# Linear attention with complex decay before a mixture of experts: the state increment computed transposed, two heads in two column halves

## The chip, the cores and the metric

The kernel runs on one core of one Trainium2 chip. The metric is the device time of one execution, in microseconds (us); several executions are taken, and the median is given. Lower is better.

## What is computed

For 4 sequences (B) of 768 steps (S) and 8 heads (H) of width 48 (D), a complex state of 48x48 per head decays and takes in an outer product at each step, and a query reads its real part. The result, 3072 rows of 384 numbers, then goes through four experts with weights per row.

```python
mag = np.sqrt(a_re * a_re + a_im * a_im)
scale = np.minimum(mag, 0.999) / (mag + 1e-06)
a_re_n, a_im_n = (a_re * scale, a_im * scale)
for t in range(S):
    ar, ai = (a_re_n[:, :, t, :, None], a_im_n[:, :, t, :, None])
    new_re = ar * S_re - ai * S_im
    new_im = ar * S_im + ai * S_re
    kv = np.einsum('bhd,bhe->bhde', k[:, :, t], v[:, :, t])
    S_re, S_im = (new_re + kv, new_im)
    y[:, :, t] = np.einsum('bhd,bhde->bhe', q[:, :, t], S_re)
...
for e in range(E):
    h = np.maximum(x @ w1[e], 0.0)
    out += p[:, e:e + 1] * (h @ w2[e])
```

All data is fp32, and there are 3072 rows, 384 columns, 1024 hidden units per expert.

## The kernel before

The work has two parts that overlap in time. The rows are cut into 12 groups (g) of 256 steps, three for each sequence, and each group into two chunks (c) of 128 steps.

**Attention, per group.** VectorE normalises the decays (`norm`), forms their running products (`prefix`) and from them Q and K, the queries and keys scaled by these products (`finish`). Q and K go to DRAM and come back in another layout as `Qst` and `Kst` (SyncE's queue), with the real part in partitions 0 to 47 and the imaginary part from 64 on (M = 112 partitions, 16 between them zero). Then, per chunk, the function `chunk` hands out pieces:

- `increment`: what the chunk adds to the state. K of the chunk (one tile for the real, one for the imaginary part, i) is turned by six transposes on TensorE into `ktp` (L399), evicted by ScalarE into `KT` (L400), and multiplied with the values `vc`, one product per head, into `dp` (L404), in PSUM. The old state less `dp` is the new state `G` (L407 for the first chunk of a sequence, L409 otherwise). The last chunk of a sequence has no increment, so there are 20.
- `scores`: `Kst` times `Qst`, eight heads in two tiles `sc` (L416), masked on VectorE into `scs` (L419).
- `values`: state times queries (L428) plus scores times values (L432), into `yp`; here two heads stand in one PSUM tile, one in partitions 0 to 47, one from 64 on, which is to say that their products use two column halves of the array. ScalarE evicts `yp` (L438).

`rotate` (L450 to L453) multiplies the state by the group's whole decay on VectorE, ready for the next group.

`attention` is a generator that strings these pieces together and yields twice before its last one: increment and scores of chunk 0; its values and the scores of chunk 1; then the values of chunk 1, the store of y to DRAM and its load as the next input `xa`, the increment of chunk 1, and `rotate`.

**Experts.** Two of the four (E1) run in the first part, on the group before (`moe1`, in eight steps f2 of two blocks of 128 hidden units each). A step multiplies with the first weights into `ph` (L147), evicts it as a rounded part `hh` on ScalarE (L154) and a remainder `hl` on VectorE (L155), and multiplies those with the second weights into `po` (L164), one step later. The input is split likewise into `xha` (ScalarE, L136) and `xla` (VectorE, L137). The other two experts run in a second part on all rows (`phb` L568, `pob` L581), after the attention is done.

**What sets the order.** A scheduler orders the instructions of each engine by its own estimates of time. The program's text gives the priorities: `between` takes the next piece of `attention` at steps k of the experts' loop, and `first` says from which on. Instructions under `keep_in_program_order` stay in the order of the text. PSUM tiles of the attention (`ktp`, `dp`, `sc`, `yp`) share four buffers, tag `pa`.

Of the kernel before, what the change touches and what calls it, by code (L numbers as in the profile page):

```python
# [8 lines left out]
F32 = mybir.dt.float32  # L9
F32R = mybir.dt.float32r  # L10
AF = mybir.ActivationFunctionType
ALU = mybir.AluOpType
# [3 lines left out]
B, H, S, D = 4, 8, 768, 48  # L16
HD = H * D
NT = B * S
E, F = 4, 1024
P = 128  # L20
# [3 lines left out]
CG = G // C  # L24
# [9 lines left out]
M = 112  # L34
IM = 64
# [24 lines left out]
def fast_path(ctx, tc, qkP, aP, vP, probsP, w, out, flag):  # L60
# [134 lines left out]
    with ExitStack() as c1:  # L195
# [18 lines left out]
        KT = big.tile([P, H, M], F32, name="KT")  # L214
# [5 lines left out]
        nc.gpsimd.memset(KT, 0.0)  # L220
# [163 lines left out]
        def chunk(g, c, K, y):  # L384
# [8 lines left out]
            def increment():  # L393
                if last:
                    return
                for i in range(2):
                    kt_ps = ps_a.tile([P, HD], F32, tag="pa", name=f"ktp{g}_{c}_{i}")
                    for j in range(NJ):
                        nc.tensor.transpose(kt_ps[:, j * P:(j + 1) * P], K[:, i, j * CG + c, :], ident)  # L399
                    nc.scalar.activation(KT[:, :, i * IM:i * IM + D],  # L400
                                         kt_ps.rearrange("p (h d) -> p h d", d=D), AF.Copy)
                d_ps = ps_a.tile([M, H, D], F32, tag="pa", name=f"dp{g}_{c}")
                for h in range(H):
                    nc.tensor.matmul(d_ps[:, h, :], KT[:, h, :], vc[:, h * D:(h + 1) * D], start=True, stop=True)  # L404
                Gt = small.tile([M, H, D], F32, tag="G", name=f"G{g}_{c}")
                if first:
                    nc.scalar.activation(Gt, d_ps, AF.Copy, scale=-1.0)  # L407
                else:
                    nc.vector.tensor_tensor(Gt, state[g, c], d_ps, op=ALU.subtract)  # L409
                state[g, c + 1] = Gt  # L410
# [29 lines left out]
            return increment, scores, values  # L440
# [15 lines left out]
        def attention(g, K):  # L456
            y = small.tile([M, HP, G], F32, tag="y", name=f"y{g}")
            (inc0, sc0, val0), (inc1, sc1, val1) = (chunk(g, c, K, y) for c in range(CG))
            inc0()
            yield sc0()  # L460
            if g == 0:
                sc1()
            val0()
# [8 lines left out]
            inc1()  # L472
            rotate(g)
            yield x
# [41 lines left out]
        x = {0: split_x(0, [r for r in attention(0, K.pop(0))][-1])}  # L516
        for g in range(NG + 1):
            if g == NG:
                check_all()
            if g >= 1:  # L520
# [3 lines left out]
                def between(k, g=g, pieces=pieces, first=first):  # L524
                    if first <= k < first + 3:
                        r = next(pieces, None)
                        if r is not None:
                            x[g] = r
# [278 lines left out]
```

## Time and profile before

| | us |
|---|---|
| median of three runs | 1034.55 (1033.19 to 1038.9) |
| the profiled execution, its own time | 1037.87 |
| its span in the trace | 1036.2 |
| PE busy in the span | 995.4 |
| DVE busy | 597.5 |
| ACT busy | 360.6 |
| increments (L404), PE busy, x320 | 35.7 |
| transposes of K (L399), PE busy, x120 | 19.1 |
| eviction into KT (L400), ACT busy, x40 | 18.4 |
| subtraction into G (L409), DVE busy, x16 | 8.9 |
| scores (L416), PE busy, x384 | 54.5 |
| values (L428 and L432), PE busy, x320 and x384 | 32.1 and 36.1 |

PE is TensorE's multiplying, PEld its loading of weights, which overlaps; DVE is VectorE, ACT ScalarE, POOL GpSimd, SP SyncE. Rows of matmuls count passes: a product of two fp32 operands shows as two records, a transpose as one. A record's duration includes the way through the array, so several overlap, and the distance between starts tells what one costs. Rows of a timeline give start, duration, engine, line, operation, tiles (output <- inputs), operand sizes and a count of merged records; in square brackets the idle time before, with what ended it.

### The profile page before, as it was taken

Reading aid. Unit: us, or ns where it says so; the run is one execution under the profiler, and the core shown is the slowest. Engines: PE = TensorE matmul, PEld = TensorE weight load, DVE = VectorE, ACT = ScalarE, POOL = GpSimd, SP = SyncE. Lnnn points to the kernel's source line nnn. Section 1 sums busy time; section 2 is a strip of 40 time slices with the busy share of each in tenths; the row PEclk is TensorE's granted clock in tenths of the full one; section 3 lists DMA queues with packets and bytes.
Section 4 is the critical chain, followed back from the end, with each engine's and each line's share of the span. In section 5 each row is a group of like instructions: output and inputs, shape, how many; then the busy total and the mean of one; then the engine's idle time right before and its main releaser. Section 6 shows DMA issues by size and latency. Waiting matters only on the chain.

```text
span 1036.2 us, 15971 instructions
## 1 busy us (share of the span) xinstructions
PE 995.4 (96%) x6522; PEld 926.2 (89%) x6522; DVE 597.5 (58%) x1195; ACT 360.6 (35%) x647; POOL 25.2 (2%) x47
## 2 busy tenths in 40 slices
PE   5689999899999999999999999999999999999996
PEld 3469899898999999999999999999999999999996
DVE  6688888797978898888982264232232232321221
ACT  7745345262534626355342254121111111111110
POOL 4000000000000000000000000000000000000000
PEclk9689999899999999999999999999999999999999
DMA  8826373564638455483652493012030010100000
GB/s 281 206 100 139 110 203 112 149 160 116 182 111 206 121 147 150 118 212 119 146 132 68 130 358 123 1 38 85 1 109 14 23 70 1 61 1 1 31 1 34
DMA packets 80722, 113.12 MB, mean 109 GB/s; under 512 B 5440, under 2 KB 66032, under 8 KB 80640
## 3 DMA queue, kind: packets, MB, share of 16 engines
q1 hardware_dynamic: 78368, 102.40, 35.8%
q0 software_dynamic: 2272, 9.62, 2.6%
q8 instruction: 53, 0.87, 0.4%
q14 instruction: 29, 0.24, 0.1%
HBM read 74.11 MB, written 37.88 MB: 108 GB/s over the span
## 4 chain that ended last, share of the span: by engine, by line
PE 84%; DMA 7%; DVE 5%; ACT 2%; issue 1%; DVEq 0%; POOL 0%; SPq 0%; ACTq 0%; POOLq 0%
PE pob L581 19%; PE phb L568 19%; PE ph L147 16%; PE po L164 15%; PE sc L416 5%; DMA Kst<-k_d 2%; PE yp L432 2%; PE lp L123 2%; PE dp L404 2%; PE yp L428 2%; DMA k_d<-K 2%; PE ktp L399 1%; DMA xa<-y_d 1%; DMA pr<-probsP 1%; DMA y_d<-y 1%
## 5 line engine op out<-in xcount | busy, mean ns | idle before, releaser
L574 DVE SCALAR_TENSOR_TENSOR hlb<-phb,hhb 128x512 fp32r<-128x512 f32 x96 | 66.3, 691 | 245.5 <-ACT hhb L573 245.5
L573 ACT ACTIVATE hhb<-phb 128x512 fp32r<-128x512 f32 x96 | 57.4, 598 | 313.3 <-PE phb L568 299.1
L164 PE MATMUL po<-wlo,hh 128*128 128x384 f32 x384 | 129.4, 337 | 0.0
L581 PE MATMUL pob<-wlo,hhb 128*128 128x384 f32 x384 | 129.3, 337 | 0.0
L164 PE MATMUL po<-whi,hh 128*128 128x384 f32 x384 | 129.1, 340 | 0.0
L581 PE MATMUL pob<-whi,hhb 128*128 128x384 f32 x384 | 128.9, 336 | 0.0
L164 PE MATMUL po<-whi,hl 128*128 128x384 f32 x384 | 123.6, 338 | 0.6 <-DVE hl L155 0.6
L581 PE MATMUL pob<-whi,hlb 128*128 128x384 f32 x384 | 117.8, 336 | 0.0
L154 ACT ACTIVATE hh<-ph 128x512 fp32r<-128x512 f32 x96 | 57.2, 596 | 158.2 <-PE ph L147 154.8
L147 PE MATMUL ph<-xha,whi 128*128 128x256 f32 x576 | 105.0, 290 | 5.3 <-ACT xha L136 5.3
L147 PE MATMUL ph<-xha,wlo 128*128 128x256 f32 x576 | 104.2, 287 | 0.0
L147 PE MATMUL ph<-xla,whi 128*128 128x256 f32 x576 | 102.7, 286 | 0.0
L155 DVE SCALAR_TENSOR_TENSOR hl<-ph,hh 128x512 fp32r<-128x512 f32 x96 | 66.0, 688 | 54.6 <-ACT hh L154 54.2
L147 PEld LDWEIGHTS ph<-xha,whi 128*128 128x128 f32 x576 | 87.6, 194 | 6.3 <-ACT xha L136 5.7
L568 PE MATMUL phb<-xhb,whi 128*128 128x512 f32 x288 | 91.8, 392 | 0.0
L147 PEld LDWEIGHTS ph<-xha,wlo 128*128 128x128 f32 x576 | 85.1, 194 | 0.4 <-issue 0.4
L147 PEld LDWEIGHTS ph<-xla,whi 128*128 128x128 f32 x576 | 83.9, 193 | 0.7 <-issue 0.7
L568 PE MATMUL phb<-xlb,whi 128*128 128x512 f32 x288 | 83.4, 392 | 0.0
L568 PE MATMUL phb<-xhb,wlo 128*128 128x512 f32 x288 | 82.1, 393 | 0.0
L581 PEld LDWEIGHTS pob<-wlo,hhb 128*128 128x128 f32 x384 | 72.1, 188 | 3.5
L581 PEld LDWEIGHTS pob<-whi,hhb 128*128 128x128 f32 x384 | 72.1, 188 | 3.4
L164 PEld LDWEIGHTS po<-whi,hh 128*128 128x128 f32 x384 | 72.6, 189 | 0.2 <-issue 0.2
(201 smaller groups left out, 1576.2 us busy)
## 6 DMA issues: line engine op xcount, KB each, us to landing
wst<-w SPq DMA_DIRECT2D x32, 384.0 KB, 5.2
qk<-qkP SPq DMA_DIRECT2D x24, 384.0 KB, 7.1
acc_d<-acc POOLq DMA_DIRECT2D x24, 384.0 KB, 4.4
prev<-acc_d SPq DMA_DIRECT2D x24, 384.0 KB, 4.8
q_d<-Q SPq DMA_DIRECT2D x22, 387.0 KB, 4.1
Qst<-q_d SPq DMA_DIRECT2D x22, 387.0 KB, 6.0
A<-aP SPq DMA_DIRECT2D x22, 384.0 KB, 8.4
k_d<-K SPq DMA_DIRECT2D x22, 384.0 KB, 2.9
```

The lines of the kernel that those rows point to most:

```text
L123: nc.tensor.matmul(lp, ident, src[:, us], start=True, stop=False)
L147: ins = nc.tensor.matmul(ph[:, u, :], wt[:, j * P:(j + 1) * P], xt[:, j, :], start=(n == 0), stop=(n == 3 * NJ - 1))
L154: nc.scalar.activation(hh, ph, AF.Relu)
L155: nc.vector.scalar_tensor_tensor(hl, ph, 0.0, hh, op0=ALU.max, op1=ALU.subtract)
L164: nc.tensor.matmul(po[t], ht[:, u, t * P:(t + 1) * P], wt[:, HD:], start=(i % FE == 0 and n == 0), stop=(i % FE == FE - 1 and n == 2))
L404: nc.tensor.matmul(d_ps[:, h, :], KT[:, h, :], vc[:, h * D:(h + 1) * D], start=True, stop=True)
L416: nc.tensor.matmul(s_ps[:, h, :], Kc[:, hf * 4 + h, :], Qc[:, hf * 4 + h, :], start=True, stop=True)
L428: ins = nc.tensor.matmul(yo, state[g, c][:, h, :], Qc[:, h, :], start=True, stop=False)
L568: nc.tensor.matmul(ph, wt[:, j * P:(j + 1) * P], xt[:, j, :], start=(n == 0), stop=(n == 3 * NJ - 1))
L573: nc.scalar.activation(hh, ph, AF.Relu)
L574: nc.vector.scalar_tensor_tensor(hl, ph, 0.0, hh, op0=ALU.max, op1=ALU.subtract)
L581: nc.tensor.matmul(po[t], ht[:, t * P:(t + 1) * P], wt[:, HD:], start=(i % FE == 0 and n == 0), stop=(i % FE == FE - 1 and n == 2))
```

## The change

The increment changes sides. Before, K was the operand that is loaded into the array (128 steps by 112 columns: real part, zeros, imaginary part) and the head's values streamed (48 columns); the result stood as the state does, d in partitions, e along the row. Now the values are loaded (48 columns), and K streams, 48 real and 48 imaginary columns of a head side by side; the result is the transposed increment. Two heads share a PSUM tile, one in partitions 0 to 47 and one from 64 on, like the values' products. ScalarE evicts both halves into a tile `dT`, and four transposes on TensorE, one per head pair, turn it into `zp`, from which the subtraction reads.

The transposes and the subtraction are a piece of their own, `turn`: for chunk 0 it comes after the scores, for chunk 1 after one more `yield`, so that a group now takes four steps of the experts' loop (`first + 4`) instead of three, with `rotate` in the fourth.

```diff
-        KT = big.tile([P, H, M], F32, name="KT")
+        KT = big.tile([P, 2, HD], F32, name="KT")
+        dT = big.tile([M, HP, 2, IM], F32, name="dT")
...
-        nc.gpsimd.memset(KT, 0.0)
+        nc.gpsimd.memset(dT, 0.0)
...
-                    nc.scalar.activation(KT[:, :, i * IM:i * IM + D],
-                                         kt_ps.rearrange("p (h d) -> p h d", d=D), AF.Copy)
-                d_ps = ps_a.tile([M, H, D], F32, tag="pa", name=f"dp{g}_{c}")
-                for h in range(H):
-                    nc.tensor.matmul(d_ps[:, h, :], KT[:, h, :], vc[:, h * D:(h + 1) * D], start=True, stop=True)
+                    nc.scalar.activation(KT[:, i], kt_ps, AF.Copy)
+                d_ps = ps_a.tile([P, HP, 2, D], F32, tag="pa", name=f"dp{g}_{c}")
+                for p in range(HP):
+                    for u, h in enumerate((2 * p, 2 * p + 1)):
+                        ins = nc.tensor.matmul(d_ps[u * IM:u * IM + D, p], vc[:, h * D:(h + 1) * D],
+                                               KT[:, :, h * D:(h + 1) * D], start=True, stop=True)
+                        if p or u:
+                            tc.keep_in_program_order(ins)
+                for u in range(2):
+                    us = slice(u * IM, u * IM + D)
+                    nc.scalar.activation(dT[us, :, :, :D], d_ps[us], AF.Copy)
+
+            def turn():
+                if last:
+                    return
+                z_ps = ps_a.tile([M, HP, P], F32, tag="pa", name=f"zp{g}_{c}")
+                for p in range(HP):
+                    nc.tensor.transpose(z_ps[:, p, :M], dT[:, p].rearrange("q c d -> q (c d)")[:, :M], ident[:M, :M])
+                zv = z_ps.rearrange("q p (u e) -> q (p u) e", u=2)[:, :, :D]
                 Gt = small.tile([M, H, D], F32, tag="G", name=f"G{g}_{c}")
                 if first:
-                    nc.scalar.activation(Gt, d_ps, AF.Copy, scale=-1.0)
+                    nc.scalar.activation(Gt, zv, AF.Copy, scale=-1.0)
                 else:
-                    nc.vector.tensor_tensor(Gt, state[g, c], d_ps, op=ALU.subtract)
+                    nc.vector.tensor_tensor(Gt, state[g, c], zv, op=ALU.subtract)
...
             inc0()
             yield sc0()
             if g == 0:
                 sc1()
+            turn0()
             val0()
...
             inc1()
+            yield x
+            turn1()
             rotate(g)
-            yield x
+            yield None
...
-                    if first <= k < first + 3:
+                    if first <= k < first + 4:
```

Since the scheduler places the instructions anew, others move too. Three places follow; a row is line, operation, output <- inputs, size and count, and lines of the changed kernel from L399 on stand one, later up to 18 lines further down.

On PE, around the scores of group 2, chunk 0, which run among the expert steps of group 1 (the number after `hh`, `hl` and `ph` is the step f2). Before:

```order
L164 MATMUL po_0_1_1347<-whi_420,hh_3_1477 128x384
L164 MATMUL po_0_1_1347<-wlo_421,hh_3_1477 128x384
L404 MATMUL dp_0_1433<-v_0_1419,KT 112x48 x8
L416 MATMUL sc_0_0_1444<-Qst,Kst 128x128 x4
L416 MATMUL sc_0_1_1451<-Qst,Kst 128x128 x4
L428 MATMUL yp_0_1493<-Qst,G_1_1111 48x128 x2
L164 MATMUL po_0_1_1347<-whi_420,hl_3_1478 128x384
L147 MATMUL ph_5_1594<-xha_1152,whi_473 128x256 x3
```

and with the change:

```order
L164 MATMUL po_0_1_1376<-wlo_370,hh_1_1396 128x384
L164 MATMUL po_0_1_1376<-whi_369,hl_1_1397 128x384
L405 MATMUL dp_0_1462<-KT,v_0_1448 48x96 x3
L431 MATMUL sc_0_0_1473<-Qst,Kst 128x128 x4
L431 MATMUL sc_0_1_1480<-Qst,Kst 128x128 x4
L147 MATMUL ph_3_1487<-xha_1181,whi_408 128x256 x3
L147 MATMUL ph_3_1487<-xha_1181,wlo_409 128x256 x3
L147 MATMUL ph_3_1487<-xla_1182,whi_408 128x256 x3
```

The scores stand behind step 3's second product before, and behind step 1's now; the eight increments are cut into five (further up) and three, with the experts' `po` between.

On PE, ahead of the values of group 8, chunk 0. Before:

```order
L164 MATMUL po_0_1_4503<-whi_368,hh_1_4523 128x384
L164 MATMUL po_0_1_4503<-wlo_369,hh_1_4523 128x384
L164 MATMUL po_0_1_4503<-whi_368,hl_1_4524 128x384
L428 MATMUL yp_0_4614<-Qst,G_1_4191 48x128 x2
L432 MATMUL yp_0_4614<-scs_0_0_4570,v_0_4540 48x128 x2
L428 MATMUL yp_0_4614<-Qst,G_1_4191 48x128 x2
```

and with the change:

```order
L164 MATMUL po_0_1_4602<-wlo_370,hh_1_4622 128x384
L164 MATMUL po_0_1_4602<-whi_369,hl_1_4623 128x384
L418 MATMUL zp_0_4713<-ident,dT 112x112 x4
L443 MATMUL yp_0_4720<-Qst,G_1_4331 48x128 x2
L447 MATMUL yp_0_4720<-scs_0_0_4669,v_0_4639 48x128 x2
L443 MATMUL yp_0_4720<-Qst,G_1_4331 48x128 x2
```

The four transposes `zp` stand directly ahead of the values; the products that they turn were issued before the two tiles of scores, one whole `ph` and `po` further up.

On DVE, at the start of the experts on group 0. `xla` is the input's remainder for the first expert step, `hl_0` that step's eviction; `sk_16`, `fm1` and `A` belong to `prefix` of group 1, `Q` to its `finish`, `s` is a sum of squares in it, and `G` with `P` is `rotate`. Before:

```order
L453 TENSOR_TENSOR G_1_660<-G_1_660,P_163 112x384
L137 TENSOR_TENSOR xla_667<-xa_639,xha_666 128x768
L266 TENSOR_TENSOR A_187<-sk_16a,sk_16b 128x3x16
L267 TENSOR_TENSOR A_187<-sk_16a,sk_16b 128x3x16
L262 TENSOR_TENSOR fm1a<-A_187 128x651
L264 TENSOR_TENSOR fm1a<-A_187 128x651
L263 TENSOR_TENSOR fm1b<-A_187 128x651
L265 TENSOR_TENSOR fm1b<-A_187 128x651
L155 SCALAR_TENSOR_TENSOR hl_0_806<-ph_0_786,hh_0_805 128x512
L266 TENSOR_TENSOR A_187<-fm1a,fm1b 128x21x31
L267 TENSOR_TENSOR A_187<-fm1a,fm1b 128x21x31
L155 SCALAR_TENSOR_TENSOR hl_1_831<-ph_1_811,hh_1_830 128x512
```

and with the change:

```order
L263 TENSOR_TENSOR fm1a<-A_188 128x651
L265 TENSOR_TENSOR fm1a<-A_188 128x651
L264 TENSOR_TENSOR fm1b<-A_188 128x651
L266 TENSOR_TENSOR fm1b<-A_188 128x651
L468 TENSOR_TENSOR G_1_675<-G_1_675,P_164 112x384
L137 TENSOR_TENSOR xla_682<-xa_647,xha_681 128x768
L267 TENSOR_TENSOR A_188<-fm1a,fm1b 128x21x31
L268 TENSOR_TENSOR A_188<-fm1a,fm1b 128x21x31
L345 ISA s_759,st_a_158<-s_759 128x24x16
L345 ISA st_a_158 128x1
L345 ISA s_759,st_a_158<-s_759 128x24x16
L345 ISA st_a_158 128x1
```

The four `fm1` products stood behind `xla` and stand ahead of it now. Directly after the last row shown come the two rows of `Q`, and only then `hl_0`, which stood between the `fm1` products and the sums before.

More of the change, by code (lines that the diff above doesn't have):

```diff
@@ L438, in values @@
                     nc.scalar.activation(y[us, :, cs], y_ps[us], AF.Copy)
-            return increment, scores, values
+            return increment, turn, scores, values
         def rotate(g):
@@ L457, in attention @@
             y = small.tile([M, HP, G], F32, tag="y", name=f"y{g}")
-            (inc0, sc0, val0), (inc1, sc1, val1) = (chunk(g, c, K, y) for c in range(CG))
+            (inc0, turn0, sc0, val0), (inc1, turn1, sc1, val1) = (chunk(g, c, K, y) for c in range(CG))
             inc0()
@@ L515, in fast_path @@
             split_w(i, stage1(i, PRE), ps_o, la)
-        x = {0: split_x(0, [r for r in attention(0, K.pop(0))][-1])}
+        x = {0: split_x(0, [r for r in attention(0, K.pop(0)) if r is not None][-1])}
         for g in range(NG + 1):
```

## The prediction

> **What bounds the kernel now.** I read the page's busy shares first, then its slices, then a table of stretches, then the waits.
>
> ```profile
> PE 995.4 (96%) x6522; PEld 926.2 (89%) x6522; DVE 597.5 (58%) x1195; ACT 360.6 (35%) x647; POOL 25.2 (2%) x47
> PE   5689999899999999999999999999999999999996
> DVE  6688888797978898888982264232232232321221
> PEclk9689999899999999999999999999999999999999
> ```
>
> TensorE (PE) is busy nearly everywhere, but busy is no proof that it sets the pace. VectorE (DVE) is near full in the same slices 3 to 21, and nearly idle after. So the program has stages, and I ask for them:
>
> ```profile
> core 0: us, PE busy (x) PEld busy (x) DVE busy (x) ACT busy (x) POOL busy (x), PEclk, DMA share, GB/s
> 74.00:290.00 216.00, 206.14 (x1579) 198.95 (x1580) 181.39 (x374) 95.22 (x173) 4.39 (x8) 0.95 0.56 147
> 290.00:577.00 287.00, 287.00 (x2358) 280.66 (x2357) 227.64 (x487) 125.88 (x236) 6.51 (x12) 1.00 0.52 134
> 625.00:1036.00 411.00, 403.18 (x2031) 365.86 (x2029) 112.99 (x164) 69.61 (x113) 0.54 (x1) 0.99 0.11 36
> ```
>
> Stage I (74 to 290 us): PE idles 9.9 us, and its clock is granted at 0.95. Stage II (290 to 577): PE never idles, at full clock; a us of PE work less is a us less, as long as nothing else is late. From 577 on no attention is left, and the change touches nothing there. The waits of stage I, as releaser, total us, count and longest:
>
> ```profile
> PE sc L416 <- DMA Kst<-k_d: 6.3, 3, 3.1
> ...
> PE ph L147 <- ACT xha L136: 5.3, 2, 3.4
> ```
>
> The first is the chain that DVE sets: DVE finishes K of a group, K goes to DRAM and comes back as Kst, and the scores wait for it. The second is the expert phase waiting for its input; 3.4 us of it is the very start. And a wait costs more than itself:
>
> ```profile
> 285.80:287.00 1.20, 0.04 (x1) 0.07 (x1) 1.02 (x2) 0.00 (x0) 0.00 (x0) 0.96 1.01 338
> 287.00:290.40 3.40, 3.40 (x17) 3.40 (x17) 1.02 (x3) 0.00 (x0) 0.00 (x0) 0.51 0.68 261
> ```
>
> After 1.2 us of idleness the clock stood at half for 3.4 us, so about 1.7 us more was lost. By the Trainium skill, "TensorE: Matmul & The Clock Gate", section "HAM oscillation — how this bites in real kernels", only idle gaps of more than about 3.4 us are to be avoided; by that rule this wait would have cost 1.2 us, by the row it cost 2.9, and I go by the row.
>
> **The change, part by part.** The increment goes first: eight products per chunk, twenty chunks (the last of each batch has none).
>
> ```profile
> 212.24 0.52 PE L147 MATMUL ph<-xha,whi 128*128 128x256 f32 x3
> 212.59 1.68 PE L404 MATMUL dp<-v,KT 128*112 128x48 f32 x16
> 214.10 0.42 PE L164 MATMUL po<-whi,hh 128*128 128x384 f32 x1
> 214.35 0.34 PE L164 MATMUL po<-wlo,hh 128*128 128x384 f32 x1
> ```
>
> Sixteen records are eight products in two passes each. From the first start (212.59) to the second po start, less one po pitch of 0.18 us, the block occupies 1.58 us, 98 ns a pass, though only 48 columns stream: the 112-column load sets it. This goes. What comes is written like the value products, two heads in two column halves:
>
> ```profile
> 206.15 0.35 PE L164 MATMUL po<-whi,hl 128*128 128x384 f32 x1
> 206.33 0.34 PE L164 MATMUL po<-whi,hh 128*128 128x384 f32 x1
> 206.60 0.43 PE L432 MATMUL yp<-scs,v 128*48 128x128 f32 x4
> 206.86 0.39 PE L428 MATMUL yp<-Qst,G 112*48 112x128 f32 x4
> 207.08 0.39 PE L432 MATMUL yp<-scs,v 128*48 128x128 f32 x4
> ...
> 207.96 0.39 PE L432 MATMUL yp<-scs,v 128*48 128x128 f32 x4
> 208.28 0.55 PE L399 MATMUL ktp<-ident,K 128*128 128x128 f32 x3
> ```
>
> Four records take 0.22 us (206.86 to 207.08), so a pass of both halves takes 0.11 us at 128 streamed columns. The new products stream 96. In proportion that is 0.083 us, at worst the same 0.11. Four pairs of two passes are 0.66 us a chunk, up to 0.88. I take 0.66: loading 2x48 columns at the old block's rate, 98 ns for 112 columns, comes to 84 ns too.
>
> The same rows show a price that is easily missed. po to po is 0.18 us (206.15 to 206.33), but po to the first yp is 0.27: entering costs 0.09. The last four yp should end 0.22 after 207.96, at 208.18, and ktp starts at 208.28: leaving costs 0.10. I charge 0.18 to each block of new products. The Trainium skill, "TensorEngine Tiling (Array Packing)", section "Key Properties", says that a change of tiling mode drains TensorE, without a figure; it speaks against this change, whose old products stood in the neighbours' mode. If instead the 0.09 were a wait for the yp data, the sum below would be -8.7 us; with the drain it is -4.2.
>
> By the order of instructions the products stand in 27 blocks, not 20: seven chunks are cut in two, four of these inside a pair, whose products then run one after the other (two passes of 0.083 more, 0.17 us). Then the transposes, whose nearest rows are those of K:
>
> ```profile
> 183.15 0.34 PE L164 MATMUL po<-wlo,hh 128*128 128x384 f32 x1
> 183.32 0.82 PE L399 MATMUL ktp<-ident,K 128*128 128x128 f32 x6
> 183.89 0.59 PE L164 MATMUL po<-whi,hl 128*128 128x384 f32 x2
> 184.32 0.34 PE L164 MATMUL po<-whi,hh 128*128 128x384 f32 x1
> ```
>
> Six transposes, a single pass each, occupy 183.32 to 184.32 less two po pitches (0.35), 0.65 us, 0.108 each. Four narrower ones (112 columns) take 0.38 to 0.43; I take 0.40. They stand just ahead of a yp block, so they enter no mode of their own.
>
> PE work per chunk: -1.58 + 0.66 + 0.40 = -0.52. The first two chunks lie before 74 us, where PE waits for loads, and I count nothing there. The other 18: -9.4; their 25 blocks +4.5; the four cut pairs +0.7. **Sum -4.2 us**; with 0.88 for the products -0.2 us; with blocks free at both sides -8.7.
>
> **ScalarE** gets two evictions more per chunk, 48 partitions by 384 elements.
>
> ```profile
> L400 ACT ACTIVATE KT<-ktp 128x384 f32<-128x384 f32 x40 | 18.4, 488 | 8.7 <-PE ktp L399 8.4
> ```
>
> By this row of as many elements 0.49 us each, 40 of them: 20 us. In stages I and II it is busy 95.22 of 216 and 125.88 of 287 us, so there is room; I cost them at nothing. The cover is that an expert step's eviction has a whole step of PE work ahead of its use. If that were gone, 1 us a chunk would show, 18 us in all. The KT eviction keeps its size, the subtraction on DVE too. The memset on GpSimd is off every path.
>
> **What is late next.** The state now waits for products, two evictions, four transposes and the subtraction. The transposes are the wait that is added: behind them PE holds the values of the same chunk, and ScalarE's eviction of the values, the store of y and the next group's input come after. By the order at least 3.5 us of other PE work stands between products and transposes from group 1 on, against 1.0 us of evictions, so I cost this wait at nothing; uncovered it would be 1 us a chunk. But the order on DVE shifts, and this is where I had to choose. At the start:
>
> ```profile
> 73.94 1.01 PE L147 MATMUL ph<-xha,whi 128*128 128x256 f32 x3 [3.39 <-ACT xha L136]
> ...
> 76.66 0.84 PE L147 MATMUL ph<-xla,whi 128*128 128x256 f32 x3
> ```
>
> ```profile
> 70.58 0.56 DVE L409 TENSOR_TENSOR G<-G,dp 112x384 f32<-112x384 f32 x1 [1.00 <-PE dp L404]
> ...
> 74.20 0.95 DVE L137 TENSOR_TENSOR xla<-xa,xha 128x768 fp32r<-128x768 f32 x1
> ...
> 75.30 0.84 DVE L262 TENSOR_TENSOR fm1a<-A 128x651 f32<-128x651 f32 x1
> 76.05 0.83 DVE L264 TENSOR_TENSOR fm1a<-A 128x651 f32<-128x651 f32 x1
> ...
> 79.84 0.69 DVE L155 SCALAR_TENSOR_TENSOR hl<-ph,hh 128x512 fp32r<-128x512 f32 x1 [1.46 <-ACT hh L154]
> ```
>
> The order shown above puts four fm1 products (0.75 us apart, 3.0 us) ahead of xla, and Q of group 1 ahead of the first hl. xla would end at 78.2; PE reads it at 76.66 and loses 1.5 us; for the first hl I allow 1 us more, 2.5 in all. DVE gets on with K of group 1 instead, and no longer idles 1.46 us for hh. Scores of groups 1 to 4 move forward on PE past one or two expert steps, which brings them to Kst too early; K moves forward on DVE too (group 2's ahead of three hl, 3 x 0.69 = 2.1 us). The 2.5 us at the start, and at worst as much again in one new wait with its slow clock, stand against the 6.3 us of Kst waits and their slow clock (three times 1.7), which may go. Bounds +5 and, 11.4 less 2.5, -9. Neither end has a row that decides it; the waits that go are about as many as those that come, so I take **0**.
>
> In stage II the Kst chain has little slack:
>
> ```profile
> Kst<-k_d SPq DMA_DIRECT2D x22, 384.0 KB, 5.8
> ```
>
> ```profile
> 367.00 1.43 SPq L371 DMA_DIRECT2D Kst<-k_d  x2
> ...
> 376.20 2.02 PE L416 MATMUL sc<-Qst,Kst 112*128 112x128 f32 x16
> ```
>
> The second of two issues goes out at about 368.1, lands 5.8 later at 373.9, and PE takes it at 376.2: 2.3 us of slack. So PE may be 2.3 us earlier before it waits here. The ten chunks of stage II save less than that: -5.2, 16 blocks +2.9, three cut pairs +0.5, -1.8 us. It holds if DVE is not later itself.
>
> **The forecast.** The profiled execution took 1037.87 us, of which the span is 1036.2: less 4.2 it is 1033.7. It stood 3.3 above the median of the runs, 1034.55; against that median it is **1030 us**, -0.4%. A measurement of this kernel can tell about 0.5%, 5.2 us, from no change, so this is just inside.
>
> **The rivals.**
> - *Stage I eats its share.* There PE waits for Kst, so a faster PE only waits longer. Then stage II's -1.8 is all: 1032.7. For it: the waits for Kst, DVE busy 181 of 216 us. Against: expert work moves behind these waits, and may fill them less or more than before.
> - *The waits of stage I go.* Scores that stand elsewhere meet a Kst that has landed; beside the -4.2, half of the bound of 9: 1026. For it: K ahead of three evictions on DVE. Against: the scores move forward as well.
> - *DVE's loop becomes the bound of stage II (slower).* From K over Kst and scores back to the next K a round takes about 46 us (503 us of both stages over eleven groups). The subtraction of a group's first half stood ahead of scs (rows below), in time that DVE spends until Kst lands anyway; now it stands behind, on the way to the next K. That is 0.56 us, with up to two hl (0.69) in its train 1.9 a round: over five rounds 9.7, less the slack of 2.3, less stage II's 1.8, with nothing from stage I: +5.6, 1040. It decides once a round's DVE work grows by more than 0.5 us (2.3 over five). Against: DVE has idle time, 59 of 287 us.
>
> ```profile
> 376.40 0.56 DVE L409 TENSOR_TENSOR G<-G,dp 112x384 f32<-112x384 f32 x1 [0.31 <-PE dp L404]
> ...
> 377.36 0.69 DVE L419 TENSOR_TENSOR scs<-sc,maskp 128x512 f32<-128x512 f32 x1
> ```
>
> - *The halves don't overlap in the new products* (the change doesn't do what it says): 16 passes at 83 ns are 1.33 us, +0.67 on 18 chunks, +12.0 less 4.2: 1042. Against: four yp records in 0.22 us are 55 ns each, half of a transpose's 108 that streams the same 128 columns.
>
> **How the numbers follow.** Forecast 0.40 (1027 to 1033, four tenths of it faster by over 0.5%), stage I eats its share 0.20, waits go 0.22, DVE's loop 0.13, no overlap 0.05. Faster 0.16 + 0.22 = 0.38; same 0.24 + 0.20 = 0.44; slower 0.18. The range: 0.88 for the products (1034) lies inside; above it reaches into the loop's cases, below to 1022, near the full bound of the waits: 1022 to 1039. Out of it stay no overlap, about half of the loop's cases and the best of the waits, 0.15.
>
> **What would show it.** A block of eight new products at 0.66 us, with 0.09 at each side, and four transposes at 0.40: the PE sum. The waits of scores for Kst in stage I in all near 6 us, the clock near 0.95: the zero. PE without idle time from 290 on: the slack. Wrong it is if the products take 0.11 a pass, if scores wait for Kst in stage II, or if hh stands behind the new evictions.

## The result

The changed kernel takes 1045.47 us (median of four runs, 1045.06 to 1045.95), beside 1034.24 us for the kernel before in runs on the same chip: a ratio of 1.0109, interval 1.0082 to 1.0136. In a later set of runs it was 1.0154 (1.0123 to 1.0186). So it is slower, by a little over 1% and clear of the noise, against a forecast of 1030 us and a range that ended at 1039. The profiled execution (1045.06 us, span 1043.3) is 7.1 us longer in its span than that of before; the medians are 11.2 us apart, so the two traces show only a part of the loss.

The page of the changed kernel:

```profile
PE 991.4 (95%) x6602; PEld 914.6 (88%) x6602; DVE 596.8 (57%) x1195; ACT 378.1 (36%) x687; POOL 24.8 (2%) x47
PE   6589979999999999899999999999999999999997
DVE  6678798888888888688883265223233232321221
PEclk9788989999999999899999999999999999999999
```

PE is busy for 4.0 us less, and the kernel is longer: the time went into standing still. The same table of stretches as in the prediction says where:

```profile
74.00:290.00 216.00, 200.72 (x1616) 192.27 (x1617) 182.82 (x379) 104.07 (x191) 4.37 (x8) 0.96 0.56 146
290.00:577.00 287.00, 281.40 (x2325) 270.32 (x2324) 226.74 (x485) 131.82 (x251) 6.47 (x12) 0.99 0.51 135
625.00:1036.00 411.00, 410.75 (x2083) 373.43 (x2081) 114.96 (x166) 72.85 (x118) 0.54 (x1) 1.00 0.11 38
```

PE idles 15.3 us in stage I (9.9 before) and 5.6 in stage II (none before): 11.0 more. The clock has to be counted with it. In the traces it stands at half for 17.1 us of stage I (21.4 before) and for 6.8 us of stage II (0.3 before). If half of PE's busy time at half clock is taken as lost, which is an estimate, idle time and slow clock together cost 21.1 us in stage I, where it was 19.7 before, and 8.2 us in stage II, where it was 0.2. So nearly all of the loss that these traces show lies in stage II. PE's waits in both stages together, total us, count and longest:

```profile
PE ph L147 <- DVE xla L137: 7.0, 2, 6.4
PE sc L431 <- issue: 6.4, 4, 3.9
PE sc L431 <- DMA Kst<-k_d: 4.3, 4, 1.4
PE ph L147 <- ACT xha L136: 3.8, 1, 3.8
```

Two things are new: a wait of 6.4 us for the experts' input `xla`, and waits of the scores in stage II. ("issue" before `sc` is the same wait for Kst: the longest, before 426.04, ends as a transfer into Kst lands, 12.0 us after the end of K.) A round in stage II, group 8, on PE, then on SyncE's queue, where K goes to DRAM and comes back, and on DVE:

```profile
421.75 0.37 PE L405 MATMUL dp<-KT,v 128*48 128x96 f32 x4
426.04 3.75 PE L431 MATMUL sc<-Qst,Kst 112*128 112x128 f32 x16 [3.91 <-issue]
429.44 0.99 PE L147 MATMUL ph<-xha,whi 128*128 128x256 f32 x3
```

```profile
413.13 1.25 SPq L368 DMA_DIRECT2D k_d<-K  x2
417.82 1.21 SPq L372 DMA_DIRECT2D Kst<-k_d  x2
```

```profile
412.16 1.82 DVE L361 TENSOR_TENSOR K<-A,u 128x768 f32<-128x768 f32 x2
...
422.34 0.56 DVE L301 TENSOR_TENSOR pf<-A 128x384 f32<-128x384 f32 x1
428.12 0.69 DVE L434 TENSOR_TENSOR scs<-sc,maskp 128x512 f32<-128x512 f32 x1 [5.22 <-PE sc L431]
428.73 0.25 DVE L303 TENSOR_TENSOR A<-pf 128x96 f32<-128x96 f32 x1
...
433.27 0.69 DVE L155 SCALAR_TENSOR_TENSOR hl<-ph,hh 128x512 fp32r<-128x512 f32 x1 [1.23 <-ACT hh L154]
...
435.11 0.55 DVE L424 TENSOR_TENSOR G<-G,zp 112x384 f32<-112x384 f32 x1 [0.22 <-PE zp L418]
```

DVE takes its instructions in order here. It stands 5.22 us at the masked scores, though the next group's prefix (`pf` and `A`, started before and resumed after) needs nothing from them. That work, and with it the next K, comes late; so does the next Kst, and so the next scores. Between the end of K (413.98) and the masked scores it had run 7 instructions of that prefix. In the same round before, it came to the masked scores with 15 of them done:

```profile
422.54 0.55 DVE L409 TENSOR_TENSOR G<-G,dp 112x384 f32<-112x384 f32 x1 [0.31 <-PE dp L404]
423.02 0.25 DVE L302 TENSOR_TENSOR A<-pf 128x96 f32<-128x96 f32 x1
423.18 0.25 DVE L303 TENSOR_TENSOR A<-pf 128x96 f32<-128x96 f32 x1
423.50 0.69 DVE L419 TENSOR_TENSOR scs<-sc,maskp 128x512 f32<-128x512 f32 x1
```

DVE's waits at the masked scores in stage II, before and then changed, sum it up:

```profile
DVE scs L419 <- PE sc L416: 8.0, 12, 3.8
```

```profile
DVE scs L434 <- PE sc L431: 20.4, 17, 5.2
```

### The profile page after: what moved, and what is told of

It reads as the page before. It is cut to its first block, busy times and chain, and to the rows that moved or that the text cites. A ratio compares the mean times of both kernels' runs of the same rounds, so it can differ in the third digit from the quotient of the medians.

```text
span 1043.3 us, 16202 instructions
## 1 busy us (share of the span) xinstructions
PE 991.4 (95%) x6602; PEld 914.6 (88%) x6602; DVE 596.8 (57%) x1195; ACT 378.1 (36%) x687; POOL 24.8 (2%) x47
## 4 chain that ended last, share of the span: by engine, by line
PE 79%; DMA 8%; DVE 7%; ACT 3%; issue 2%; SPq 1%; ACTq 0%; DVEq 0%
PE pob L599 19%; PE phb L586 19%; PE ph L147 14%; PE po L164 14%; PE sc L431 5%; DMA Kst<-k_d 3%; PE yp L447 2%; DMA k_d<-K 2%; PE yp L443 2%; DMA q_d<-Q 1%; PE dp L405 1%; PE ktp L400 1%; DVE K L361 1%; PE lp L123 1%; DMA A<-aP 1%
## 5 line engine op out<-in xcount | busy, mean ns | idle before, releaser
L154 ACT ACTIVATE hh<-ph 128x512 fp32r<-128x512 f32 x96 | 57.3, 596 | 147.4 <-PE ph L147 146.9
```

The source lines that it names most:

```text
L154: nc.scalar.activation(hh, ph, AF.Relu)
```

## The experiments

The question was which part of the change makes PE and DVE stand: the two evictions, the turn's place, the fourth piece, or the order that the scheduler makes of them. The table gives each ratio to the kernel before on the same chip with its interval, PE's idle time in stages I and II (216 and 287 us less the busy time), and DVE's waits for the scores at `scs` in stage II.

| kernel | ratio | PE idle I + II, us | `scs` waits II, us |
|---|---|---|---|
| before | 1 | 9.9 + 0 | 8.0 |
| changed | 1.0109 (1.0082 to 1.0136) | 15.3 + 5.6 | 20.4 |
| changed again (e11) | 1.0154 (1.0123 to 1.0186) | 18.2 + 5.3 | 14.9 |
| e1, turns in the increments | 0.9902 (0.9872 to 0.9933) | 2.2 + 0 | 4.0 |
| e1 again (e12) | 0.9904 (0.9886 to 0.9921) | 3.2 + 0.1 | 4.0 |
| e2, old products, new pieces | 0.9977 (0.9961 to 0.9993) | 9.5 + 0 | 7.6 |
| e3, before with evictions | 1.0009 (0.9986 to 1.0031) | 10.2 + 1.6 | 8.8 |
| e4, changed, one eviction | 1.0058 (1.0028 to 1.0088) | 18.3 + 3.1 | 14.9 |
| e5, first turn early | 0.9940 (0.9915 to 0.9964) | 8.6 + 1.1 | 2.6 |
| e6, second turn early | 1.0127 (1.0087 to 1.0167) | 15.2 + 7.5 | 15.0 |
| e7, subtraction behind `scs` | 0.9982 (0.9960 to 1.0004) | 8.6 + 1.3 | 12.2 |
| e8, e1 with one eviction | 0.9920 (0.9895 to 0.9945) | 3.6 + 0.7 | 3.8 |
| e9, prefix held, more | 1.0028 (1.0008 to 1.0047) | 10.4 + 0.6 | 13.8 |
| e10, prefix held, less | 1.0002 (0.9985 to 1.0019) | 11.8 + 0 | 10.6 |
| e13, changed, pieces later | 0.9982 (0.9966 to 0.9999) | 12.0 + 0.7 | 10.0 |
| e14, before, pieces later | 1.0002 (0.9982 to 1.0022) | 7.8 + 1.0 | 6.5 |

**e1: both turns inside the increments.** Everything of the new product stays; `turn` loses its own place, and a group has three pieces again.

```diff
-
-            def turn():
-                if last:
-                    return
...
-            turn0()
...
-            yield x
-            turn1()
             rotate(g)
-            yield None
+            yield x
...
-                    if first <= k < first + 4:
+                    if first <= k < first + 3:
```

> The changed kernel's arithmetic (transposed products, two evictions, four transposes), but turned back and subtracted inside the increment, with the three pieces per group of the kernel before; so DVE's subtraction stands ahead of the masked scores again. By instruction order the DVE work between the last masked scores and the next K falls to 122 us over rounds 7 to 10 (134 in the changed kernel, 128 before). Theory order (the separate turn puts DVE work into the loop K, Kst, scores, next K): 1030 to 1036 us, and K of the last groups no later than before. Theory evictions (the two new evictions stand in ScalarE's queue ahead of what DVE's loop waits for): all 36 evictions are still there, so 1041 to 1047 us with the same late K.

1027.68 us, 0.9902: faster than both kernels, and a little below the band of the theory of order. The theory of evictions falls here already. The stretches of e1:

```profile
74.00:290.00 216.00, 213.77 (x1731) 202.69 (x1731) 188.83 (x400) 106.38 (x196) 4.37 (x8) 0.98 0.57 148
290.00:577.00 287.00, 287.00 (x2356) 274.15 (x2356) 221.04 (x462) 135.14 (x255) 7.02 (x13) 1.00 0.54 137
```

No scores wait for Kst any more, in either stage. The run also gives the price of a block that nothing cuts:

```profile
119.75 0.34 PE L164 MATMUL po<-whi,hh 128*128 128x384 f32 x1
120.02 0.87 PE L405 MATMUL dp<-KT,v 128*48 128x96 f32 x16
120.82 0.44 PE L164 MATMUL po<-wlo,hh 128*128 128x384 f32 x1
121.10 0.33 PE L164 MATMUL po<-whi,hl 128*128 128x384 f32 x1
```

Counted as the old block was, from 120.02 to 121.10 less one pitch of 0.18, it is 0.90 us, and entering costs 0.09 more: 0.99, where 0.84 was forecast. The sides cost what was forecast (0.19 for 0.18); the sixteen passes take 0.80 us for 0.66. A block that is cut costs more than its share. In the changed kernel, twelve passes of a chunk:

```profile
418.39 0.52 PE L147 MATMUL ph<-xla,whi 128*128 128x256 f32 x3
418.84 0.70 PE L405 MATMUL dp<-KT,v 128*48 128x96 f32 x12
419.47 0.44 PE L164 MATMUL po<-whi,hh 128*128 128x384 f32 x1
419.75 0.34 PE L164 MATMUL po<-wlo,hh 128*128 128x384 f32 x1
```

With both sides this is 0.83 us, and four passes alone take 0.50 (at 561.56 us), so a chunk cut into twelve and four takes 1.33 us; one cut into ten and six takes 1.48. Of the changed kernel's eighteen chunks eleven are whole, three are cut the first way and four the second: 20.8 us in all. With eighteen times 0.40 for the transposes that is 28.0, against 28.6 for the old products: PE saves 0.6 us. In stage II, where six of the ten chunks are cut, it saves nothing (16.4 us for 15.9). In e1 fifteen are whole, and it saves 1.9 us.

So most of e1's gain is not the cheaper product. In stages I and II its PE idles 7.7 us less than before and loses an estimated 5.9 us less to the half clock; with the 1.9 that is 15.5 us, where the span of 1024.5 is 11.7 shorter, so some 4 us stay unexplained. In the changed kernel the same sum (11.0 more idle, 1.7 less lost to the clock, 0.6 less work) is 8.7 us, and the span is 7.1 longer.

**e2: the old product in the new pieces.** The reverse: products, tiles and eviction as before, the subtraction alone in `turn`.

```diff
+                dps.append(d_ps)
...
             def turn():
                 if last:
                     return
-                z_ps = ps_a.tile([M, HP, P], F32, tag="pa", name=f"zp{g}_{c}")
-                for p in range(HP):
-                    nc.tensor.transpose(z_ps[:, p, :M], dT[:, p].rearrange("q c d -> q (c d)")[:, :M], ident[:M, :M])
-                zv = z_ps.rearrange("q p (u e) -> q (p u) e", u=2)[:, :, :D]
+                zv = dps[0]
```

> The products, tiles and evictions of the kernel before, but the subtraction in a piece of its own behind the scores, and four pieces per group as in the changed kernel. Theory order: loses what the changed kernel loses and lacks the cheaper products, so 1043 to 1050 us. Theory evictions: no new eviction, so as before, 1033 to 1037 us.

0.9977: the theory of order misses. A piece more per group and a subtraction written later cost nothing alone; in the instruction order the subtraction stands where it stood, since its products are ready there. What e2 lacks of the turn are the transposes; that they are what keeps the turn behind the scores is argued, not shown.

**e3: before, with two evictions that nobody reads.**

```diff
                     nc.tensor.matmul(d_ps[:, h, :], KT[:, h, :], vc[:, h * D:(h + 1) * D], start=True, stop=True)
+                for u in range(2):
+                    us = slice(u * IM, u * IM + D)
+                    nc.scalar.activation(dT[us, :, :, :D], d_ps[us].rearrange("p (a b) d -> p a b d", b=2), AF.Copy)
```

> The kernel before with two more ScalarE evictions of each increment's products into a tile that nothing reads; products, pieces and subtraction as before. Theory evictions: the loss without the cheaper products, 1041 to 1050 us, with K of the last groups 8 to 11 us later than before. Theory order: 1033 to 1037 us as before. By instruction order the evictions also move DVE work into the round (134 us over rounds 7 to 10 against 128), so a third theory, that the evictions act through the order that the scheduler makes of it, expects 1038 to 1042: only the 6 us of work, without longer waits for ScalarE.

1038.42 us, where before took 1037.6 on the same chip: 1.0009. In time that would fit the third theory, as a ratio it doesn't; the evictions cost nothing here. The DVE work from the masked scores to the end of the next K did grow (durations of 133.0 us in rounds 7 to 10, 127.0 before), but the span is 1036.4, with 1.6 us of idle PE in stage II: PE still set the pace.

**e4: the changed kernel with one eviction per chunk.** A product takes 64 columns of values, 16 of them another head's or zero, so that one eviction covers both halves.

```diff
-                        ins = nc.tensor.matmul(d_ps[u * IM:u * IM + D, p], vc[:, h * D:(h + 1) * D],
+                        ins = nc.tensor.matmul(d_ps[u * IM:(u + 1) * IM, p], vw[:, h * D:h * D + IM],
...
-                for u in range(2):
-                    us = slice(u * IM, u * IM + D)
-                    nc.scalar.activation(dT[us, :, :, :D], d_ps[us], AF.Copy)
+                nc.scalar.activation(dT[:, :, :, :D], d_ps[:M], AF.Copy)
```

> The changed kernel with 64 columns of values per product pass instead of 48 (the extra 16 are other heads' or zero columns), so that a single eviction of 112 partitions takes the place of two of 48: 18 evictions of about 0.49 us fewer. Theory evictions: half or more of the loss goes, 1036 to 1041 us. Theory order: the pieces are those of the changed kernel, 1043 to 1047 us.

1045.33 us on a chip where before took 1037.6, so 1.0058. In time it is what the theory of order expected, as a ratio about half of the loss, so by itself it decides nothing. Its waits are much like the changed kernel's: 6.55 us for `xla`, and 14.9 us at `scs` in stage II, as in e11. But its ratio lies below both of the changed kernel's, and its interval reaches into the first (1.0082 to 1.0136) and not into the second (1.0123 to 1.0186). So in this order the second eviction may carry up to half of the loss, or the order, which differs a little too; e8 tests it only with the turns early.

**e5 and e6: one of the two turns early.** e5 puts chunk 0's turn ahead of its scores and leaves chunk 1's in the fourth piece; e6 is the other half. First e5, then e6:

```diff
             inc0()
+            turn0()
             yield sc0()
             if g == 0:
                 sc1()
-            turn0()
```

```diff
             inc1()
-            yield x
             turn1()
             rotate(g)
-            yield None
+            yield x
...
-                    if first <= k < first + 4:
+                    if first <= k < first + 3:
```

> The changed kernel with the turn of a group's first chunk directly behind its products, ahead of the scores; the second chunk's turn stays in a piece of its own, four pieces per group. The first subtraction stands ahead of the masked scores again, and by instruction order the DVE work from the masked scores to the next K falls to 117 us over rounds 7 to 10 (134 changed, 122 with both turns early). Theory first turn (the turn behind the scores is what puts DVE work into the loop): 1024 to 1031 us, no wait of scores for Kst from 290 us on, K of the last groups 6 us or more earlier than before. Theory pieces (the fourth piece delays the rotation and the next group's increments): 1036 us or more.

> The changed kernel with the second chunk's turn in the increment and three pieces per group; the first chunk's turn stays behind the scores. By instruction order 138 us of DVE work from masked scores to next K over rounds 7 to 10. Theory first turn: as slow as the changed kernel or slower, 1041 to 1050 us, with DVE standing 3 us or more at the masked scores. Theory pieces: 1028 to 1035 us.

1032.49 us (0.9940) and 1052.26 us (1.0127): it is the first turn, the one behind the scores. In time they lie 1.5 and 2.3 us above their bands; before took 1038.71 us on that chip, 4.5 more than beside the changed kernel, and as ratios both fit. In e5 K of the last groups came at most 5.5 us earlier, less than expected, and in group 11 1.4 us later. Of e5's idle time 6.32 us are a single wait for `xla`, which the changed kernel has too. There, first on PE, then on DVE:

```profile
131.27 0.52 PE L147 MATMUL ph<-xha,wlo 128*128 128x256 f32 x3
138.17 1.01 PE L147 MATMUL ph<-xla,whi 128*128 128x256 f32 x3 [6.38 <-DVE xla L137]
```

```profile
131.01 0.55 DVE L424 TENSOR_TENSOR G<-G,zp 112x384 f32<-112x384 f32 x1
...
136.70 0.55 DVE L468 TENSOR_TENSOR G<-G,P 112x384 f32<-112x384 f32 x1
137.17 0.95 DVE L137 TENSOR_TENSOR xla<-xa,xha 128x768 fp32r<-128x768 f32 x1
```

and in e1, on DVE:

```profile
124.12 0.96 DVE L137 TENSOR_TENSOR xla<-xa,xha 128x768 fp32r<-128x768 f32 x1 [0.49 <-ACT xha L136]
...
127.09 0.55 DVE L420 TENSOR_TENSOR G<-G,zp 112x384 f32<-112x384 f32 x1
```

In group 1 the pieces start at step 4, so the fourth falls into step 7, where the input is split; `xla` is kept in program order and so stands behind the turn and the rotation. e5's span is 6.7 us above e1's, and this one wait with the 6.8 us at half clock around its end is enough for that. No run moves the fourth piece of group 1 alone, so whether it costs anything elsewhere is not shown.

**e7: the subtraction alone behind the masked scores.** e2, with chunk 0's subtraction tied behind both `scs`.

```diff
-                    nc.vector.tensor_tensor(Gt, state[g, c], zv, op=ALU.subtract)
+                    ins = nc.vector.tensor_tensor(Gt, state[g, c], zv, op=ALU.subtract)
+                    if c == 0:
+                        behind(ins, masked[-1])
```

> Old products without new evictions or transposes, subtraction in a piece of its own as in the earlier run, and in each group that has one the first chunk's subtraction is held behind both of its masked scores on DVE. Only 0.56 us a round moves; the rest of DVE's order stays within 1 us a round (128 us over rounds 7 to 10). Theory position (the subtraction's own place behind the masked scores costs the loop): 1039 us or more. Theory work ahead of the wait (what counts is how much other DVE work stands between K and the masked scores, and here that stays): as before within 0.4%, 1031 to 1040 us.

0.9982: with the old products its place costs nothing. The third rival of the prediction had this as its first term.

**e8: e1 with one eviction**, by the edit of e4.

> Both turns in the increment with three pieces (the fastest so far) and a single eviction of 112 partitions per chunk in place of two. If ScalarE's evictions cost nothing once DVE's loop is not the bound: the same as with two, 1024 to 1031 us, 0.986 to 0.994 of before. If they still cost (the transposes wait for both, 0.97 us a chunk): 4 us or more faster than with two, below 1023 us.

0.9920 beside 0.9902 and 0.9904: 18 evictions fewer gain nothing where the turns are early. The run shows one thing more: with 64 loaded columns of values in place of 48 the block of products with both its sides takes 1.00 us, where it was 0.99. So the number of loaded columns hardly counts in these products, though the prediction took 0.66 us also from the old block's rate per loaded column.

**e9 and e10: only DVE's prefix work held back.** In the kernel before, the next group's prefix from step 4 (e9) or 5 (e10) on is tied behind the first masked scores.

```diff
+                if i >= 4 and g - 1 in masked:
+                    behind(ins, masked[g - 1])
```

> The kernel before, nothing changed but DVE's order: from its fourth step on, the next group's prefix chain may not start ahead of the first masked scores. By instruction order 9 instructions of that chain or fewer then stand ahead of the masked scores in every round (10 to 17 before, 7 to 13 in the changed kernel), and 137 us of DVE work from masked scores to next K over rounds 7 to 10 (128 before, 134 changed). Theory work ahead of the wait (DVE stands at the masked scores until Kst has landed; work taken from ahead of them comes late): DVE's idle time at the masked scores 33 us or more (26.4 before, 34.1 changed), and 1041 to 1048 us, 1.003 to 1.010 of before. Theory new work (only the evictions, transposes and the turn itself cost): as before, 0.997 to 1.003.

> As the run beside it, but held from the fifth step on: at most 12 instructions of the chain ahead, which changes rounds 6 to 10 alone, by 3 to 5 short instructions (about 1 us) each; 133 us over rounds 7 to 10. Theory work ahead of the wait: about half of the other run's loss or less, since scores have some 2 us of slack there, 0.998 to 1.005 of before, idle time at the masked scores 27 to 32 us. Theory new work: 0.997 to 1.003, idle time 26 us.

1.0028 and 1.0002. The group of masked scores in e9, with DVE's idle time ahead of it behind the second bar:

```profile
L422 DVE TENSOR_TENSOR scs<-sc,maskp 128x512 f32<-128x512 f32 x48 | 33.1, 689 | 30.1 <-PE sc L419 27.8 <-PE yp L437 2.3
```

The direction is right and the size isn't: 30.1 us, where 33 or more was expected, and a ratio just below the band, inside that of new work, though its interval (1.0008 to 1.0047) excludes a ratio of 1. In e10 the idle time is 28.0 us, as the first theory has it, and the ratio fits both. e9 puts as much work behind `scs` as the changed kernel (durations of 136.0 us in rounds 7 to 10, there 133.2) for about 3 us. On PE the scores hardly wait (0.6 us in stage II, 5.6 there). So late DVE work alone, in this amount, does not explain the loss either.

**e11 and e12** repeat the changed kernel and e1 on one chip: 1052.01 and 1027.5 us.

> The changed kernel once more, beside the others on one chip: 1.008 to 1.014 of before.

> Both turns inside the increments, once more, on the same chip as the changed kernel: 0.986 to 0.994 of before, 16 to 22 us below the changed kernel.

1.0154 is a little above its band and 0.9904 inside; they stand 24.5 us apart, more than expected.

**e13: the changed kernel, its pieces one step later; e14: the same in the kernel before.** In the instruction order the first scores of group 7 have 1488 expert passes ahead of them on PE before, 1488 in the changed kernel and 1529 in e1. That suggested that the scores themselves stand too early. The edit is one number in both, and changes the groups from the third on (for group 2, `5 - g` is 3 already):

```diff
-                first = max(2, 5 - g)
+                first = max(3, 5 - g)
```

> The changed kernel, its turn behind the scores as it is, but from group 2 on the four pieces of a group stand one expert step later. From group 4 on 30 or so more expert passes (240 a round) stand on PE ahead of a group's first scores, about as in the fast kernel with both turns in the increments (1518 ahead of group 7's, 1529 there, 1488 in the changed kernel and before), and 115 us of DVE work from masked scores to next K over rounds 7 to 10 (134 changed). Group 1 stays as it is, with its wait of some 6 us for xla. Theory early scores (the scores reach Kst too early, PE and DVE both stand there, and with them the loop): 0.988 to 0.999 of before although the turn is where it was, no wait of scores for Kst over 0.5 us from 330 us on, DVE's idle time at the masked scores below 22 us. Theory turn (the late products, transposes and subtraction themselves): 1.008 to 1.016.

> The kernel before, with the pieces one expert step later from group 3 on. There scores waited little for Kst from 330 us on, so theory early scores expects nothing in stage II and at most the two or three last waits of stage I, 0.993 to 1.001 of before. If later pieces are worth as much here as in the changed kernel (0.985 or less), the place of the scores is a gain of its own and explains nothing about the turn.

0.9982 and 1.0002, both as the theory of early scores has it; DVE's idle time at the masked scores is 21.4 us, just under the 22 expected. With the turn where it was, the loss is gone. PE's waits of scores in stage II, in e13:

```profile
PE sc L431 <- DMA Kst<-k_d: 0.5, 1, 0.5
PE sc L431 <- issue: 0.2, 1, 0.2
```

and the control shows that later scores are no gain of their own where PE does not wait for Kst. What e13 still lacks against e1 is mostly the 6.6 us wait for `xla` in group 1 and the half clock behind it.

Two things limit what e13 shows. Its edit moves the scores on PE and with them the masked scores on DVE, so DVE's work behind them falls too. And e6 speaks against the place on PE as the whole cause: there the first scores of group 7 have 1521 expert passes ahead of them, nearly as many as in e1, and still scores wait for Kst, 7.0 us in stage II.

**The loop, measured in the traces.** From K of group 6 to K of group 11 the loop goes round five times. It has two legs: from a group's first masked scores to the end of the next K, on DVE, and from the end of K over Kst and the scores to the masked scores. Both as sums over the five rounds, in us, with DVE's busy time in the first:

| kernel | masked scores to next K | of it DVE busy | K to masked scores |
|---|---|---|---|
| before | 158.4 | 137.5 | 61.2 |
| changed | 170.8 | 146.0 | 59.6 |
| changed again (e11) | 171.6 | 146.0 | 58.0 |
| e6 | 169.9 | 147.4 | 58.7 |
| e4 | 168.6 | 139.1 | 58.3 |
| e3 | 167.7 | 144.8 | 57.0 |
| e9 | 167.5 | 148.5 | 55.8 |
| e5 | 157.2 | 130.6 | 72.7 |
| e1 | 151.9 | 132.2 | 68.9 |
| e13 | 146.8 | 125.8 | 76.5 |

The second leg is at its shortest in e9, 55.8 us. PE's own five rounds, from the first scores of group 6 to those of group 11, take 226.3 us before. So, as an estimate, the first leg can grow to about 170 us before the loop sets the pace. The changed kernel, e11 and e6 have reached that, e4 nearly; e3 and e9 stay just below it; e1, e5 and e13 are far from it. By this leg e6 stands with the slow ones, as it does by its time, though not by the place of its scores on PE; it has lost most already in stage I, where K of group 6 ends 13.4 us later than before. The leg holds DVE's waits too, so its length is not the cause alone.

## Why the prediction was wrong

- **The PE sum was wrong: the blocks come to -0.6 us instead of -4.2.** Old products and transposes were sized rightly (1.58 and 0.40 us a chunk). The passes of the new products take 0.80 us for 0.66, which is 0.10 for a pass of both halves, between the 0.083 taken and the 0.11 named as the worst. And a cut costs more: 1.33 or 1.48 us a chunk, where 1.02 and 1.19 were counted.
- **Evictions at nothing: right where PE sets the pace.** e3 and e8 show it. In the changed kernel's own order e4 leaves it open.
- **The added wait at nothing: right.** In e1 the transposes stand inside the increment, the hardest case, and PE waits for evictions of `dp` only twice, 0.70 and 1.15 us, both in group 0; in the changed kernel once, 1.15 us, also there.
- **The order of stage I at 0: nearly right, by luck.** By the estimate above, idle time and slow clock grew by 1.3 us. But the 2.5 us at the start did not come (0.7 did). In their place stand 6.4 us in group 1, where the fourth piece puts the rotation ahead of `xla` and where the prediction did not look; less waiting elsewhere and less half clock made up for most of them.
- **The step that failed is stage II: "It holds if DVE is not later itself", for which the forecast set nothing aside.** The saving of 1.8 us was not there (0.5 us more PE work instead), and DVE was later: K of group 6 ends 0.9 us earlier than before, K of group 11 9.8 us later (549.6 instead of 539.8). The slack of 2.3 us was read in one group, 7; in groups 6, 8 and 9 Kst lands 0.5, 1.6 and 1.7 us ahead of the scores before.
- **The third rival had the loop right**, from K over Kst and scores back to K, and its test was met: scores wait for Kst in stage II. The leg from the masked scores to the next K grew by 12.4 us over the five rounds, 2.5 a round where the rival had 1.9; 8.5 of the 12.4 are DVE's work and 3.9 its waits. Its account of what moved does not hold as it stands: e7 moved the subtraction at no cost, and e9 put even more work behind the masked scores for 3 us.
- **What the runs put in its place.** With the first turn behind the scores, and the pieces at the old steps, DVE comes to the masked scores with less of the prefix done (7 instructions for 15 in group 8), stands there, and has more to do behind them, though its busy time in all is the same (596.8 us, 597.5 before). In e9 the first leg grew by 9.1 us, and the second gave 5.4 back, out of the time by which Kst had landed ahead of the scores. In the changed kernel the second gave back 1.6. Group 8 shows why: of PE's wait of 3.91 us, 2.9 come from a later K, 2.4 from a Kst that lands 12.0 us after K instead of 9.6 (its load goes out 3.8 us after K, 1.8 before), 0.2 from PE's earlier arrival, less the 1.6 of slack. So the cheaper product did not bring the scores forward; K and Kst came late. Expert products queue behind the waiting scores on PE, and `hl`, which needs them, holds up the prefix on DVE; that this is what makes 3.9 us of waits in the first leg, and lets K slip from round to round, fits the rows of group 8 but is argued. Early turns (e1, e5) or later pieces (e13) open the loop. Why the transfer took longer in group 8, and how the scheduler's estimates lead from the turn's place to this order, stays open.

The best kernel here is e1: the new product with the turn inside the increment, 0.990 of before.

## What to carry to other kernels

Where a transfer closes a loop between two engines that, as here, take their instructions in order, ask of a change not only how much work it adds, but what it moves behind the first instruction that waits for the transfer: work that goes from ahead of the wait to behind it lengthens the loop, though the engine's total stays the same. Read the slack of such a loop in every round and not in one. Put a new step that depends on a product next to it, and move it only with the order of the neighbours in sight. Price a block of short products by how the scheduler cuts it: here seven cuts among eighteen chunks took back most of a saving of 3.5 us. And when a piece is added to an interleaved schedule, look at the groups whose schedule is shifted: in group 1 the piece that crosses a pinned instruction made PE wait 6.3 to 6.8 us in every run that had it there with the new product.

## What the hardware showed unasked

The clock after a wait does not follow from the wait's length alone. Stretches of the changed kernel around scores that waited 3.91, 1.45 and 1.01 us (the clock is the third number from the end; the first stretch begins inside the wait, which ends at 426.04):

```profile
424.30:431.10 6.80, 5.06 (x24) 5.09 (x25) 2.26 (x6) 0.00 (x0) 0.00 (x0) 0.50 0.61 208
289.20:292.60 3.40, 3.35 (x29) 3.03 (x30) 2.19 (x6) 0.00 (x0) 0.00 (x0) 1.00 0.76 293
239.70:243.10 3.40, 3.36 (x26) 3.39 (x27) 2.19 (x6) 0.60 (x1) 0.00 (x0) 1.00 0.79 308
```

The first halved the clock for 6.8 us; the two short ones left it whole, though before a wait of 1.2 us was followed by 3.4 us at half. The Trainium skill, "TensorE: Matmul & The Clock Gate", section "HAM oscillation — how this bites in real kernels", counts only gaps above about 3.4 us. These three rows agree with it, the row of before does not, so the 1.7 us that the prediction charged for each short wait was sometimes right and sometimes too much.
